# DeltaNet followed by a capacity-limited top-1 expert layer: another way to order the tokens that every expert keeps

## The chip, the cores and the metric

The kernel runs on one core of one Trainium2 chip. The metric is the time of one execution in device microseconds. The kernel before was run three times: the median is 389.66 us (388.7 to 393.39). The profiled execution, from which all times of single instructions below are taken, has a span of 383.6 us.

## The reference

```python
# attention: q, k, v of (4, 8, 768, 48), beta of (4, 8, 768)
k_n = k / (norm(k) + 1e-6)
for t in range(S):                       # a recurrence over 768 steps per head
    y[:, :, t] = q_t @ state
    state = state + beta_t * outer(k_t, v_t - k_t @ state)
x = y as rows (3072 tokens, 384 columns)

# experts: w_gate (384, 8), w1 (8, 384, 1024), w2 (8, 1024, 384), capacity 80
logits = x @ w_gate
expert_idx = argmax(logits, axis=1)
probs = softmax(logits);  gate_w = probs[n, expert_idx[n]]
out = zeros
for e in range(8):
    tok_idx = where(expert_idx == e)
    if len(tok_idx) > capacity:          # keep the 80 with the largest gate_w
        tok_idx = tok_idx[argpartition(-gate_w[tok_idx], capacity)[:capacity]]
    h = maximum(x[tok_idx] @ w1[e], 0)
    out[tok_idx] = gate_w[tok_idx, None] * (h @ w2[e])
```

So each expert serves at most 80 tokens, those whose gate value is largest. Which tokens they are is known only when the last chunk of the recurrence has given the last logits.

## The kernel before

The recurrence runs in 12 chunks of 64 steps (j = 0 to 11). The 3072 tokens lie in 24 columns of 128. The first 16 columns (NS = 16, chunks 0 to 7) are sorted while the recurrence runs, which gives 80 kept candidates per expert ("old", tile AO with one column of values per expert). The last 8 columns (NN = 8) are "new": 4 of them early (chunks 8 and 9), 4 late (chunks 10 and 11). In the end the rank of each token among all of its expert is counted: old against old, old against new, new against old, new against new. The counts are sums of 0/1 tiles, taken on TensorE into PSUM (S_ps).

The gate of a group of columns, on VectorE (or GpSimd for the early group), with the exponential as a polynomial:

```python
def gate(m0, nm, g=nc.vector):
    ...                                   # max, shift, one-hot of the expert, range reduction
    ex = tile_(full, F32, "ex")
    g.tensor_scalar(ex, r, 1.0 / 5040.0, None, op0=Alu.mult)
    for f in (720.0, 120.0, 24.0, 6.0, 2.0, 1.0):
        stt(out=ex, in0=ex, scalar=1.0 / f, in1=r, op0=Alu.add, op1=Alu.mult)
    stt(out=ex, in0=ex, scalar=1.0, in1=two.bitcast(F32), op0=Alu.add, op1=Alu.mult)
    ...                                   # sum, reciprocal: gw, the gate value
    nc.vector.tensor_tensor(out=og, in0=oh, in1=gw..., op=Alu.mult)   # ohg: value at its expert, else 0
```

Old against old, on GpSimd, and old against new, on VectorE:

```python
            yield wide                    # ABC: AO's values as rows, on 128 partitions
            t2 = sl.tile([cap, E, cap], BF16, name="t2")
            for e in range(E):
                row, one_ = ABC[:cap, e], AO[:, e : e + 1]
                nc.gpsimd.tensor_scalar(t2[:, e], row, one_, None, op0=Alu.is_equal)
                nc.gpsimd.tensor_scalar(t1[:, e], row, one_, None, op0=Alu.is_gt)
            nc.gpsimd.tensor_tensor(out=t2, in0=t2, in1=trl[...]..., op=Alu.mult)
            nc.gpsimd.tensor_tensor(out=t1, in0=t1, in1=t2, op=Alu.add)
            after.append(lambda: nc.vector.tensor_reduce(rankO, t1, axis=AX, op=Alu.add))
            yield from against_old(early, ABC, sl)

        def against_old(ms, ABC, sl):
            for m in ms:
                G = sl.tile([128, E, cap], BF16, name="G", bufs=4)
                nc.vector.tensor_tensor(out=G, in0=ABC, in1=ohg[:, NS + m, :]..., op=Alu.is_lt)

                def sums_(m=m, G=G):
                    junk = sl.tile([128, E * cap], BF16, name="junk")
                    nc.scalar.activation(junk, G..., Act.Copy, accum_out=less[:, m : m + 1])
                    for e in range(E):
                        nc.tensor.matmul(S_ps[:cap, 1, 384 + e : 385 + e], lhsT=G[:, e, :], rhs=ones_b[:, 0:1], ...)
                counted.append(sums_)
```

New against new compares one column m with the four columns of a group, which GB holds as rows; equal values inside the own column are settled by the triangle tri:

```python
        def beats(eng, m, ms, GB, sl, own=True):
            ...
            if a:                eng.tensor_scalar(H[:, :a], GB[:, :a], g, None, op0=Alu.is_lt)
            if b < 128 * L:      eng.tensor_scalar(H[:, b:], GB[:, b:], g, None, op0=Alu.is_le)
            if b > a:            # own column: tie, then less-than plus tie
                ...
        def count(m, ms):                 # a matmul of 8 columns for each of the four
            ...
```

The last chunk and the stage after it:

```python
            if j == NC - 2:
                ...
                nc.scalar.copy(GB1, bcast_new(early))
                for m in early:
                    drain(beats(nc.gpsimd, m, early, GB1, s1))
                gate_pool(NS, NN // 2)    # rhs: the products that are gathered later
        ...
        sums(NC - 1)                      # the last logits
        for m in early:
            count(m, early)
        for f in counted:
            f()
        ...
        for i in range(WFIRST):           # 7 of 16 weight tiles
            load_w(i)
        ab, GB1 = bcast_old(), s2.tile(...)
        for h in range(2):
            nc.scalar.copy(ABC[:, 4 * h : 4 * h + 4], ab...)
        nc.scalar.copy(GB1, bcast_new(early))
        drain(gate(NS + NN // 2, NN // 2))
        gate_pool(NS + NN // 2, NN // 2)
        nc.scalar.copy(GB2, bcast_new(late))
        for m in late:
            drain(beats(nc.vector, m, early, GB1, s2))
            count(m, early)
        drain(against_old(late, ABC, s2))
        for f in counted + after:
            f()
        for m in early + late:
            drain(beats(nc.vector, m, late, GB2, s2))
            count(m, late)
        nc.vector.scalar_tensor_tensor(out=slotO, in0=S_ps[:cap, 1, 384 : 384 + E], scalar=1.0, in1=rankO, ...)
        ...                               # slots, indices idx_g and idx_s
    for e in range(E):
        gather(e)                         # rows of x by index, on GpSimd's queue
    for i in range(WFIRST, WR):           # 3 more weight tiles, once tokens are gathered
        load_w(i, ...)
    ...                                   # eight experts: w1, relu, w2, transposed back, scattered
```

PSUM tiles of this part come from `mtile()`, which hands out three buffers in rotation. The program order of each engine is the order of these calls.

Of the kernel before, what the change touches and what calls it, by code (L numbers as in the profile page):

```python
# [1 line left out]

# [18 lines left out]
ROUND = 12582912.0  # L21


@with_exitstack
def kernel(
# [126 lines left out]
    rankO = keep.tile([cap, E], F32, name="rankO")  # L152
    t1 = keep.tile([cap, E, cap], BF16, name="t1")
# [3 lines left out]
    trl = const.tile([128, 128], BF16, name="trl")  # L157
    nc.gpsimd.memset(trl, 1.0)
    nc.gpsimd.affine_select(out=trl, in_=trl, compare_op=Alu.is_gt, fill=0.0, base=0, pattern=[[-1, 128]], channel_multiplier=1)
    ioti = const.tile([128, cap], I32, name="ioti")  # L160
# [25 lines left out]
    with ExitStack() as actx:  # L186
# [416 lines left out]
        def gate(m0, nm, g=nc.vector):  # L603
# [49 lines left out]
            g.tensor_scalar(ex, r, 1.0 / 5040.0, None, op0=Alu.mult)  # L653
            yield 0.25
            for f in (720.0, 120.0, 24.0, 6.0, 2.0, 1.0):
                stt(out=ex, in0=ex, scalar=1.0 / f, in1=r, op0=Alu.add, op1=Alu.mult)
                yield 0.25
            stt(out=ex, in0=ex, scalar=1.0, in1=two.bitcast(F32), op0=Alu.add, op1=Alu.mult)
# [5 lines left out]
            nc.vector.tensor_scalar_add(sm, sm, 1e-9)  # L664
# [42 lines left out]
        def bcast_old():  # L707

            ab = mtile()
            for e in range(E):  # L710
                nc.tensor.transpose(ab[:, e // 4, (e % 4) * cap : (e % 4) * cap + cap], AO[:, e : e + 1].to_broadcast([cap, 128]),
                                    ident[:cap, :cap])
            return ab

# [6 lines left out]
        def choose_sorted(sl):  # L721
# [25 lines left out]
            W2 = [sl.tile([E, 2, 128], F32, name=f"W{i}") for i in range(2)]  # L747
# [58 lines left out]
            hots = [sl.tile([128, E, cap], BF16, name="G", bufs=4) for _ in range(NS // E)]  # L806
# [20 lines left out]
            ABC = sl.tile([128, E, cap], F32, name="ABC")  # L827

            def wide():
                ab = bcast_old()  # L830
                for h in range(2):
                    nc.scalar.copy(ABC[:, 4 * h : 4 * h + 4], ab[:, h, : 4 * cap].rearrange("p (e t) -> p e t", t=cap))

            yield wide
            t2 = sl.tile([cap, E, cap], BF16, name="t2")
            for e in range(E):
                row, one_ = ABC[:cap, e], AO[:, e : e + 1]
                nc.gpsimd.tensor_scalar(t2[:, e], row, one_, None, op0=Alu.is_equal)
                nc.gpsimd.tensor_scalar(t1[:, e], row, one_, None, op0=Alu.is_gt)
            nc.gpsimd.tensor_tensor(out=t2, in0=t2, in1=trl[:cap, :cap].unsqueeze(1).to_broadcast([cap, E, cap]), op=Alu.mult)  # L840
            nc.gpsimd.tensor_tensor(out=t1, in0=t1, in1=t2, op=Alu.add)
            after.append(lambda: nc.vector.tensor_reduce(rankO, t1, axis=AX, op=Alu.add))
            yield from against_old(early, ABC, sl)

        counted, after = [], []

        def against_old(ms, ABC, sl):

            for m in ms:
                G = sl.tile([128, E, cap], BF16, name="G", bufs=4)  # L850
                nc.vector.tensor_tensor(out=G, in0=ABC, in1=ohg[:, NS + m, :].unsqueeze(2).to_broadcast([128, E, cap]), op=Alu.is_lt)

                def sums_(m=m, G=G):
                    junk = sl.tile([128, E * cap], BF16, name="junk")
                    nc.scalar.activation(junk, G.rearrange("p e t -> p (e t)"), Act.Copy, accum_out=less[:, m : m + 1])
                    for e in range(E):
                        nc.tensor.matmul(S_ps[:cap, 1, 384 + e : 385 + e], lhsT=G[:, e, :], rhs=ones_b[:, 0:1], start=False,
                                         stop=(m == NN - 1), skip_group_check=True)

                counted.append(sums_)  # L860
                yield 0.85

        def beats(eng, m, ms, GB, sl, own=True):

            L = len(ms)
            H = sl.tile([128, NN // 2 * 128], BF16, name="H", bufs=4)[:, : 128 * L]
            g = gwN[:, m : m + 1]
            a = sum(i < m for i in ms) * 128
            b = a + 128 * (m in ms)
            if a:  # L870
                eng.tensor_scalar(H[:, :a], GB[:, :a], g, None, op0=Alu.is_lt)
                yield 0.4
            if b < 128 * L:
                eng.tensor_scalar(H[:, b:], GB[:, b:], g, None, op0=Alu.is_le)
                yield 0.4
            if b > a:
                t = sl.tile([128, 128], BF16, name="tie", bufs=2)
                if eng is nc.vector:
                    eng.scalar_tensor_tensor(out=t, in0=GB[:, a:b], scalar=g, in1=tri, op0=Alu.is_equal, op1=Alu.mult)
                    yield 0.3  # L880
                    eng.scalar_tensor_tensor(out=H[:, a:b], in0=GB[:, a:b], scalar=g, in1=t, op0=Alu.is_lt, op1=Alu.add)
                    yield 0.3
                else:
                    eng.tensor_scalar(t, GB[:, a:b], g, None, op0=Alu.is_equal)
# [407 lines left out]
```

## Time and profile before

| | |
|---|---|
| median of three runs | 389.66 us |
| span of the profiled execution | 383.6 us |
| busy: PE, DVE, ACT, POOL | 317.6, 210.0, 178.0, 211.7 us |
| last logits copied (lg) | 268.4 us |
| first weight load issued | 271.7 us |
| slots of the kept tokens (slotO) | 294.4 us |
| first gather | 299.3 us |
| last scatter issued | 379.3 us |

PE is TensorE's matmul, PEld its weight load, DVE VectorE, ACT ScalarE, POOL GpSimd. In the profile's lines, a row gives the start, the duration, the engine, the line of the kernel, the operation, what it writes and reads with shapes, the number of instructions merged into the row, and in brackets the idle time of the engine before it and what ended it. A row of waits gives who waited for whom, the time in total, how many times, and the longest. In the table of slices each digit is the busy share of a fortieth of the span in tenths.

### The profile page before, as it was taken

The numbers are of one execution on the slowest core, as the hardware profiler recorded it, in microseconds if no ns is written. First come the engines' busy times: TensorE is split into PE (matmuls) and PEld (weight loads), VectorE is DVE, ScalarE is ACT, GpSimd is POOL, SyncE is SP. The second block draws the span as 40 slices with busy tenths as digits, with TensorE's granted clock in tenths as the row PEclk, the third lists the DMA queues.
The fourth block names the chain that finished last, engine by engine and source line by source line (L and its number), as shares of the span: only waits on it lengthen the run. The fifth ranks groups of instructions, "written<-read, shape, count | busy, mean of one in ns | idle before, by whom it ended". The sixth has DMA issues, their size and how long they took to land. (4 is left out here: it accounts for less than half of the span.)

```text
span 383.6 us, 16917 instructions
## 1 busy us (share of the span) xinstructions
PE 317.6 (83%) x7356; PEld 280.6 (73%) x7356; DVE 210.0 (55%) x533; ACT 178.0 (46%) x362; POOL 211.7 (55%) x513
## 2 busy tenths in 40 slices
PE   8757869899898999798999898978633699796993
PEld 4544568799798988788999788867532399686893
DVE  7958775676247585599435769696649101010110
ACT  3644347576577676474776666553430011111110
POOL 8540786487775757582776384649994611010010
PEclk9998999899999999899999999898555889999999
DMA  9999548887897969665866566351799616999410
GB/s 139 169 165 180 98 65 167 134 169 120 172 143 152 186 104 169 120 128 103 146 109 142 86 181 138 137 192 48 281 392 388 245 43 222 394 396 392 150 26 17
DMA packets 185257, 65.29 MB, mean 170 GB/s; under 512 B 164160, under 2 KB 181568, under 8 KB 185184
## 3 DMA queue, kind: packets, MB, share of 16 engines
q1 hardware_dynamic: 156144, 56.28, 61.6%
q10 hardware_dynamic: 28272, 5.98, 8.2%
q0 software_dynamic: 768, 1.97, 1.7%
q8 instruction: 58, 0.95, 1.0%
q14 instruction: 15, 0.12, 0.1%
HBM read 44.35 MB, written 19.86 MB: 167 GB/s over the span
## 5 line engine op out<-in xcount | busy, mean ns | idle before, releaser
L415 POOL TENSOR_TENSOR tmpTrue<-XY,NT 128x14 f32<-128x14 f32 (+6 forms) x154 | 44.6, 289 | 12.1
L417 POOL TENSOR_TENSOR XY<-XY,tmpTrue 128x14 f32<-128x14 f32 (+6 forms) x154 | 41.8, 272 | 12.1
L1229 POOL DMA_INDIRECT out_dram<-y,idx_s x8 | 7.4, 921 | 63.4 <-DVE y L1228 63.4
L241 PE MATMUL pm<-SB,KQ 128*64 128x96 f32 x704 | 34.4, 249 | 2.0 <-issue 0.8
L410 POOL TENSOR_TENSOR XY<-NT,eye 128x256 f32<-128x256 f32 x11 | 9.4, 853 | 47.6 <-DMA NT<-a_blocks 42.2
L1237 PE MATMUL hp<-xTe,w 128*64 128x80 f32 x768 | 31.7, 241 | 3.9 <-issue 3.4
L539 DVE TENSOR_TENSOR UB<-pm,beta_t 64x768 f32<-64x768 f32 x24 | 22.9, 954 | 20.2 <-PE pm L241 20.0
L1237 PEld LDWEIGHTS hp<-xTe,w 128*64 128x64 f32 x768 | 29.4, 143 | 5.7 <-issue 5.0
L241 PEld LDWEIGHTS pm<-SB,KQ 128*64 128x64 f32 x704 | 30.6, 138 | 4.0 <-PE pm L241 1.9
L381 DVE TENSOR_TENSOR B<-pm,bm 128x512 f32<-128x512 f32 x24 | 16.3, 681 | 28.7 <-PE pm L241 11.6
L1228 DVE TENSOR_SCALAR y<-yp,gw_t 80x384 f32<-80x384 f32 x8 | 4.9, 613 | 49.0 <-PE yp L1226 49.0
L1250 ACT ACTIVATE hT<-hp 128x320 f32<-128x320 f32 x16 | 7.0, 437 | 52.8 <-PE hp L1237 52.8
L1237 PE MATMUL tp<-hT,w 128*64 128x80 f32 x768 | 29.6, 234 | 2.2 <-issue 1.7
L1237 PEld LDWEIGHTS tp<-hT,w 128*64 128x64 f32 x768 | 27.5, 137 | 3.8 <-issue 2.2
L241 PE MATMUL pm<-KQ 48*64 48x128 f32 x768 | 25.8, 287 | 5.0 <-ACT KQ L356 4.9
L241 PEld LDWEIGHTS pm<-KQ 48*64 48x64 f32 x768 | 22.7, 141 | 7.2 <-ACT KQ L356 6.0
L356 ACT COPY KQ<-pm 128x512 f32<-128x512 f32 x48 | 24.8, 611 | 4.8 <-issue 4.2
L467 ACT COPY X<-pm 32x256 f32<-32x256 f32 x44 | 16.0, 364 | 22.4 <-PE pm L241 18.1
L444 ACT ACTIVATE YB<-YD,qm 128x256 f32<-128x256 f32 x48 | 20.5, 499 | 11.6 <-DMA YD<-inv_blocks 11.6
L341 POOL TENSOR_TENSOR bm<-beta_t,neg_strict 128x1024 f32<-128x1024 f32 x12 | 22.8, 1900 | 1.2 <-DVE beta_t L954 1.2
L561 ACT COPY SB<-S_ps 48x768 f32<-48x768 f32 x22 | 17.5, 794 | 11.4 <-PE S_ps L241 11.2
L241 PE MATMUL pm<-R,Y 64*64 64x48 f32 x704 | 15.0, 235 | 5.2 <-issue 4.7
(258 smaller groups left out, 741.6 us busy)
## 6 DMA issues: line engine op xcount, KB each, us to landing
w<-in_moe_w_dram SPq DMA_DIRECT2D x16, 1536.0 KB, 15.9
qn<-in_q_dram SPq DMA_DIRECT2D x24, 192.0 KB, 5.4
a_blocks<-B ACTq DMA_DIRECT2D x18, 256.0 KB, 5.2
vin<-in_v_dram SPq DMA_DIRECT2D x24, 192.0 KB, 4.9
x_rows<-x SPq DMA_DIRECT2D x24, 192.0 KB, 4.0
out_dram<-zero SPq DMA_DIRECT2D x12, 384.0 KB, 4.4
kr<-in_k_dram SPq DMA_DIRECT2D x23, 192.0 KB, 4.9
inv_blocks<-XY SPq DMA_DIRECT2D x11, 256.0 KB, 2.8
```

The source lines that it names most:

```text
L241: nc.tensor.matmul(out, lhsT=lhsT, rhs=rhs, start=not acc, stop=not acc, skip_group_check=True)
L341: nc.gpsimd.tensor_tensor(out=bms[c], in0=beta_t[:, c].unsqueeze(2).to_broadcast([128, NB, 64]), in1=neg_strict.unsqueeze(1).to_broadcast( ...
L356: nc.scalar.copy(KQs[c][:, 4 * h : 4 * h + 4, n, :], pt[:, h].rearrange("r (g w) -> r g w", w=128))
L381: nc.vector.tensor_tensor(out=own(B1), in0=pv[:, 0], in1=own(bm), op=Alu.mult)
L410: eng.tensor_tensor(out=X, in0=NT.rearrange("p s t -> p t s"), in1=eye16, op=Alu.add)
L415: eng.tensor_tensor(out=tv, in0=X[:, t + 1 :, t : t + 1].to_broadcast(sh), in1=NT[:, 0:t, t].unsqueeze(1).to_broadcast(sh), op=Alu.mult)
L417: eng.tensor_tensor(out=X[:, t + 1 :, 0:t], in0=X[:, t + 1 :, 0:t], in1=tv, op=Alu.add)
L444: nc.scalar.mul(dst, Yd, w)
L467: copy(X4[hs(e, 32), :, h, e], ps[64 * e + 32 * h : 64 * e + 32 * h + 32, 0, :256].rearrange("r (g w) -> r g w", w=32))
L539: nc.vector.tensor_tensor(out=UB[hs(e), :, e].rearrange("r (g c) d -> r c g d", c=2), in0=ps[hs(e), :, : 8 * D].rearrange("r c (g d) -> r ...
L561: nc.scalar.copy(SB[hs(p, D), :, :, p].rearrange("r (b g) e d -> r b (g e) d", b=2), S_ps[hs(p, D), :, : 8 * D].rearrange("r b (g d) -> r ...
L1237: nc.tensor.matmul(out[r], lhsT=lhsT[:, r], rhs=rhs, skip_group_check=True, **kw)
```

## The change

Four things are changed, all of which concern the choice of the kept tokens.

- *Gate.* The polynomial of the exponential has a lower degree and other coefficients, scaled by a constant that is taken out again in the sum: two instructions fewer on VectorE in every gate.
- *Order of the kept tokens.* The 0/1 tiles `below` (less than; equal, times the triangle) are left apart and summed by one-column matmuls into S_ps. The addition on GpSimd, the reduction rankO on VectorE and the tile trl go. GpSimd makes them in the last chunk, ahead of the gate's products, and it makes only two of the four early comparisons; VectorE makes the other two.
- *Old against new.* In place of comparing every token with the kept values of all eight experts, the row of kept values of the token's own expert is fetched by a product: the token's one-hot column is transposed, and multiplied with the kept values, which are split into three bf16 parts (`parts`) that add up to the f32 value. One compare for four columns and one reduction follow.
- *Ties.* Each comparison of new against new is one full-width compare H; the equal values have a tile T of their own, with the triangle on the own column, and their own counting matmuls.

```diff
+EXP = (722.359314, 722.3593374, 361.1796148, 120.3915103, 30.0992743, 6.049220681)
...
-            g.tensor_scalar(ex, r, 1.0 / 5040.0, None, op0=Alu.mult)
-            for f in (720.0, 120.0, 24.0, 6.0, 2.0, 1.0):
-                stt(out=ex, in0=ex, scalar=1.0 / f, in1=r, op0=Alu.add, op1=Alu.mult)
+            for n, f in enumerate(EXP[:0:-1]):
+                stt(out=ex, in0=ex if n else r, scalar=f, in1=r, op0=Alu.add, op1=Alu.mult)
...
             def wide():
-                ab = bcast_old()
+                ab, ap = mtile(), mtile()
+                for n in range(3):
+                    nc.tensor.transpose(ap[:E, 0, cap * n : cap * n + cap], a5[:, :, 2 + n], ident[:cap, :cap])
+                nc.scalar.copy(parts, ap[:E, 0, : 3 * cap]...)
+                for e in range(E):
+                    nc.tensor.transpose(ab[:cap, ...], AO[:, e : e + 1].to_broadcast([cap, cap]), ident[:cap, :cap])
...
-                nc.gpsimd.tensor_scalar(t2[:, e], row, one_, None, op0=Alu.is_equal)
-                nc.gpsimd.tensor_scalar(t1[:, e], row, one_, None, op0=Alu.is_gt)
-            nc.gpsimd.tensor_tensor(out=t2, in0=t2, in1=trl[...]..., op=Alu.mult)
-            nc.gpsimd.tensor_tensor(out=t1, in0=t1, in1=t2, op=Alu.add)
-            after.append(lambda: nc.vector.tensor_reduce(rankO, t1, axis=AX, op=Alu.add))
-            yield from against_old(early, ABC, sl)
+                nc.gpsimd.tensor_scalar(below[0][:, e], row, one_, None, op0=Alu.is_lt)
+                nc.gpsimd.tensor_scalar(below[1][:, e], row, one_, None, op0=Alu.is_equal)
+            nc.gpsimd.tensor_tensor(out=below[1], in0=below[1], in1=tri[...]..., op=Alu.mult)
+            yield partial(own_kept, early, sl)
+            yield from against_old(early, sl)
+
+        def own_kept(ms, sl):
+            L, ot = len(ms), mtile()
+            for n, m in enumerate(ms):
+                nc.tensor.matmul(ot[:E, 0, 128 * n : 128 * n + 128], lhsT=ohN[:, m, :], rhs=identb, start=True, stop=True)
+            ohT = sl.tile([E, NN // 2 * 128], BF16, name="ohT")[:, : 128 * L]
+            nc.scalar.copy(ohT, ot[:E, 0, : 128 * L])
+            own = owns[ms[0]] = ot[:, 1, : cap * L]
+            for n in range(L):
+                for k in range(3):
+                    nc.tensor.matmul(own[:, cap * n : cap * n + cap], lhsT=ohT[:, 128 * n : 128 * n + 128], rhs=parts[:, k, :], ...)
+
+        def against_old(ms, sl):
+            G = sl.tile([128, NN // 2, cap], BF16, name="own")[:, :L]
+            nc.vector.tensor_tensor(out=G, in0=own..., in1=gwN[:, ms[0] : ms[0] + L]..., op=Alu.is_lt)
+            nc.vector.tensor_reduce(less[:, ms[0] : ms[0] + L], G, axis=AX, op=Alu.add)
+            ...                               # four matmuls of 8 columns instead of 32 of one
...
+            eng.tensor_scalar(H, GB, g, None, op0=Alu.is_le if m < ms[0] else Alu.is_lt)
+            if m in ms:
+                T = sl.tile([128, 128 * L - a], BF16, name=f"T{a}")
+                eng.tensor_scalar(T, GB[:, a:], g, None, op0=Alu.is_equal)
+                eng.tensor_tensor(out=T[:, :128], in0=T[:, :128], in1=tri, op=Alu.mult)
...
+            if j == NC - 1:
+                drain(beats(nc.vector, early[2], early, GB1, s1))
...
-                for m in early:
+                for m in early[:2]:
                     drain(beats(nc.gpsimd, m, early, GB1, s1))
-                gate_pool(NS, NN // 2)
...
+            if j == NC - 1:
+                fill(1)
+                drain(beats(nc.vector, early[3], early, GB1, s1))
+                gate_pool(NS, NN // 2)
         sums(NC - 1)
+        wide = bcast_new(early)
...
-        ab, GB1 = bcast_old(), s2.tile([128, 128 * len(early)], F32, name="GB1")
-        for h in range(2):
-            nc.scalar.copy(ABC[:, 4 * h : 4 * h + 4], ab[:, h, : 4 * cap]...)
-        nc.scalar.copy(GB1, bcast_new(early))
-        drain(gate(NS + NN // 2, NN // 2))
+        nc.scalar.copy(GB1, wide)
+        last_gate = gate(NS + NN // 2, NN // 2)
+        for _ in range(12):
+            next(last_gate)
+        own_kept(late, s2)
+        drain(last_gate)
...
-        for f in counted + after:
+        for f in counted:
             f()
+        for t in below:
+            for x in range(E):
+                nc.tensor.matmul(S_ps[:cap, 1, 384 + x : 385 + x], lhsT=t[:, x, :], rhs=ones_b[:cap, 0:1], ...)
...
-        nc.vector.scalar_tensor_tensor(out=slotO, in0=S_ps[...], scalar=1.0, in1=rankO, ...)
+        nc.vector.tensor_scalar_add(slotO, S_ps[:cap, 1, 384 : 384 + E], 1.0)
```

## The prediction

> **What bounds the kernel now.** I read the page's forty slices first, to find the stage that the change edits, then the busy time by stage, then the waits of that stage, then the instructions in order of time. The chain that ended last is no help here: it stops at the final scatter.
>
> The page, slices of 9.6 us each:
>
> ```profile
> PE   8757869899898999798999898978633699796993
> DVE  7958775676247585599435769696649101010110
> POOL 8540786487775757582776384649994611010010
> PEclk9998999899999999899999999898555889999999
> GB/s 139 169 165 180 98 65 167 134 169 120 172 143 152 186 104 169 120 128 103 146 109 142 86 181 138 137 192 48 281 392 388 245 43 222 394 396 392 150 26 17
> ```
>
> Slices 29 to 31 and part of 32 (from 268 us) are the stage between the last chunk of the recurrence and the experts: PE falls to 3 tenths and its clock to 5 while DVE and POOL work. TensorE does not bound this stage; what ends it is the choice of the kept tokens. The same stage cut at its events:
>
> ```profile
> 268.40:274.10 5.70, 2.54 (x43) 2.28 (x42) 5.04 (x24) 2.26 (x6) 5.33 (x13) 0.58 0.59 195
> 274.10:277.30 3.20, 3.20 (x24) 2.97 (x23) 0.05 (x2) 1.34 (x3) 3.20 (x8) 0.50 1.03 420
> 277.30:282.10 4.80, 3.29 (x41) 2.56 (x40) 4.80 (x8) 2.73 (x6) 4.80 (x5) 0.50 1.05 386
> 282.10:287.60 5.50, 0.72 (x9) 0.60 (x8) 0.07 (x2) 1.18 (x4) 5.42 (x9) 0.50 1.03 393
> 287.60:294.40 6.80, 2.58 (x32) 1.71 (x32) 6.41 (x19) 0.00 (x0) 4.62 (x7) 0.50 1.04 394
> ```
>
> Columns: window and length; busy time of PE, PEld, DVE, ACT, POOL; clock; DMA share; GB/s. DVE is full in rows 1, 3 and 5 and empty in rows 2 and 4. So the path is DVE's own work plus two holes of 3.2 and 5.5 us. The waits name both:
>
> ```profile
> DVE rankO L842 <- POOL t L841: 5.4, 1, 5.4
> ACT ABC L1132 <- PE pm L711: 5.1, 1, 5.1
> DVE H L871 <- ACT GB L1133: 3.1, 1, 3.1
> ```
>
> The second hole ends when POOL delivers the order of the kept tokens among themselves. The first ends when ACT has copied GB1, which stood behind ABC, whose transposes stood in PE's queue behind counts that waited for POOL's comparisons. In order of time:
>
> ```profile
> 268.38 0.18 DVE L599 COPY lg<-pm 128x16 f32<-128x16 f32 x1 [2.09 <-PE pm L597]
> ...
> 277.27 1.86 DVE L871 TENSOR_SCALAR H<-GB,gwN 128x512 bf16<-128x512 f32 x4 [3.15 <-ACT GB L1133]
> ...
> 279.05 3.07 DVE L851 TENSOR_TENSOR G<-ABC,ohg 128x640 bf16<-128x640 f32 x4
> ...
> 287.55 0.81 DVE L842 TENSOR_REDUCE rankO<-t 80x8 f32<-80x640 bf16 x1 [5.43 <-POOL t L841]
> ...
> 294.44 0.16 DVE L1148 SCALAR_TENSOR_TENSOR slotO<-S_ps,rankO 80x8 bf16<-80x8 f32 x1 [0.28 <-PE S_ps L895]
> ...
> 299.27 1.20 POOL L1203 DMA_INDIRECT xg<-x_rows,idx_g  x1 [6.76 <-DVE gw_t L1189]
> ```
>
> From the logits (268.4) to the slots (294.4) are 26.1 us, then 4.8 us to the first gather, then 79.8 us of experts to the last scatter's issue at 379.
>
> **What the Trainium skill says.** "VectorE: DVE Perf Modes", Mode 2×_2P: a single-source f32 operation between SBUF operands runs two elements a cycle, one with two tensors doesn't. The trace agrees: starts lie 0.20 us apart after a 128-wide compare against a scalar and about 0.43 after a 512-wide one, 0.6 ns an element, while the two-tensor compare of 640 takes 0.77, 1.2 ns an element. "GPSIMD Engine Reference", Key points: GpSimd shares its SBUF interfaces with VectorE and suffers from two-port or two-input DVE instructions. It agrees: POOL's 80x80 compares take 0.48 us alone and up to 1.65 beside DVE's compares; so work taken from DVE helps POOL too. "TensorE: Matmul & The Clock Gate", What's actually happening: an idle TensorE drops to half clock. It agrees, 0.50 from 274 to 299; I cost added matmuls at the pitch of that stage. "DMA: Bandwidth & Descriptors", Issuing engines are not separate DMA queues: gathers interleave with the weight stream. The first gather, issued under the stream, landed after 5.3 us against a median of 3.1.
>
> **The change part by part.**
>
> 1. *Order of the kept tokens.* The 16 compares on POOL remain but come before the gate's products, as soon as ABC exists (262.8), and not after them (274.2). POOL's own list shrinks before that: of the new tokens' comparisons only m = 0 and 1 stay with it, two times a 512-wide compare (estimate 1.6, from 1.29 for 384 and 0.93 for 256), T of 512 and 384 (1.6, 1.3) and 0.43 for the mask: 7 us, from 255.2 to about 262 where it now ends at 272.2. Then 16 x 0.48 + 1.4 = 9 us, done near 272. The sums go to 16 one-column matmuls at about 0.09 us (32 took 2.95). They are needed near 280. So the 5.43 us hole and the reduction behind it (288.29 - 287.55 = 0.74) go: **-6.17**.
> 2. *GB1.* Its transposes stand ahead of the counts, and no ABC is rebuilt in the last stage. PE and ACT make it during the gate. The hole of 3.15 shrinks to about 0.1: **-3.05**.
> 3. *Kept tokens against new ones.* Four compares of 640 (3.07) become one of 320 from PSUM and one reduction of 320. From the 256-wide PSUM addition (0.42) and the 256-wide reduction (0.42) I estimate 0.5 each: **-2.07**. ACT's four accumulations and 28 of 32 matmuls a group go as well, none on the path. The 12 products with `parts` and 4 transposes (1.3 us on PE) run during the gate.
> 4. *Gate.* Two of 23 instructions at 0.25: **-0.5**.
> 5. *Ties.* The late group's comparisons took 288.29 to 294.44, 6.15. New: 8 compares of 512 (3.45), T of 512, 384, 256 and 128 (0.45 to 0.29, sum 1.45), four products with tri (0.2 each, 0.8), PE's tail 0.4: 6.1. **0.**
> 6. *What it adds on the path.* In the last chunk TensorE does the early group's transposes and products between the output product and the transposes of x. Three transposes of a5 cost 0.5 (0.166 each, as L711). With three PSUM buffers in rotation, the extra buffer puts the product with SB onto the one that DVE's UB still reads until 262.7: it starts at 262.75 and not 261.93, +0.8 which includes the 0.5. Then x is copied (to 266.8), ACT copies ohT behind it (0.59, like GB) to 267.4, twelve products at 0.075 end at 268.3, and only then come the transposes of x, which started at 265.65: **+2.7** on the logits. Two comparisons (m = 2, 3; 1.0 us each) move to DVE, into its idle 1.54 us ahead of UB and into the wait for the logits: free.
>
> Sum: -6.17 - 3.05 - 2.07 - 0.5 + 2.7 = **-9.1 us**. Slots near 285.3, gathers near 290. Weights: the first seven tiles stream until about 302, and the next load was issued at 319.04, after the first scatter (317.85). The gap of 17 us shrinks to 8, so the tail keeps its length and moves whole.
>
> **Rivals.**
> - *PE becomes the bound at half clock*: 26 counts, 12 products, 4 + 8 transposes, some 5 us between the logits and GB2. For it: clock 0.50, in-order queue, and my plan has GB2 only about 0.5 us before its use. Against: PE idles 2 to 4 us in each window above. It would cost 2 to 3: 383.
> - *POOL stays the bound*: the products of the late tokens (rhs) start only with the gate's end and are stretched by DVE, one of them to 3.06 us today. If `below` or rhs comes late, 384 to 387. Against: 6 us of slack.
> - *The gain dies in the tail*: gathers under a full weight stream, then a colder clock in the first expert. For it: the 5.3 us. Against: that delay is already in the old run, and scatters under the stream (392 GB/s) land in 3.7. 382 to 385; whole loss unlikely.
> - *The logits aren't delayed* (part 6 hidden): 377.8.
>
> **Range and chances.** The median before is 389.66, so 380.5; the profiled span of 383.6 should become about 374.5. My uncertainty of the sum is some 3 us and the three times before spread over 4.7, so 376 to 385.5. The 2% line is at 381.9, just above my value: faster 0.68, same 0.30, slower 0.02.
>
> **What would show it.** In the new trace: no DVE wait for POOL ahead of the slots; DVE's wait ahead of the first late-by-early compare under 0.5 us; one 128x320 compare and reduction near 0.5 each; lg copied near 271, not 268.4, with PE waiting for ACT's ohT; slots near 285 and the first gather near 290; from gather to the end 80 us as before. It is wrong if PE or POOL releases DVE after the gate, or if the time from gather to end grows by more than 2 us.

## The result, and the profile after

The kernel after takes 371.02 us (median of 4 runs, 369.18 to 374.43) where the kernel before takes 389.18 (4 runs); the ratio is 0.953 [0.942, 0.963]. Predicted were 380.5, with 385.5 and 376.0 as bounds: the direction was right, the gain was twice as large as predicted. Run again on two chips, the same two kernels gave 0.962 [0.956, 0.967] (called chip A below) and 0.976 [0.969, 0.983] (chip D). That spread is itself part of the answer. The two profiled executions took 385.28 and 374.43 us and so differ by 10.9 us, the medians by 18.2.

The page of the kernel after, in slices of 9.3 us:

```profile
PE   8756978889897998897999899797767599898994
DVE  7968775775336566689462859689396001111110
POOL 8550887687574767575586277437941601010110
PEclk9999899999999999999999999879855689999999
GB/s 147 165 172 193 107 55 173 142 170 116 179 145 147 129 172 143 147 148 91 104 163 112 103 185 53 265 4 213 128 324 414 359 197 230 410 405 407 147 28 15
```

Slices 29 and 30 (270 to 289 us) hold the stage from the logits to the gathers: DVE is at 9 and 6 tenths there. Behind it, the slices in which the weight stream pauses (197 and 230 GB/s) are two, where there were 245, 43 and 222. The stage from the logits to the first gather, cut at its events (columns as before: window, length, busy PE, PEld, DVE, ACT, POOL, clock, DMA share, GB/s):

```profile
268.79:274.19 5.40, 3.23 (x49) 2.79 (x50) 4.81 (x22) 1.16 (x2) 3.87 (x11) 0.50 0.64 211
274.19:275.81 1.62, 1.62 (x21) 1.35 (x18) 1.62 (x5) 0.26 (x1) 1.23 (x4) 0.50 1.02 418
275.81:276.72 0.91, 0.65 (x11) 0.56 (x11) 0.88 (x3) 0.33 (x1) 0.46 (x2) 0.50 1.01 382
276.72:282.48 5.76, 3.85 (x59) 2.92 (x58) 5.34 (x17) 0.00 (x0) 0.00 (x0) 0.50 1.05 413
282.48:287.25 4.77, 3.19 (x21) 1.95 (x22) 3.50 (x15) 0.00 (x0) 0.00 (x0) 0.50 1.05 403
```

DVE is busy in every row. Both rows in which it was empty are gone, and POOL is idle from 276.72 on. The same in DVE's own order of time, with POOL's first gather:

```profile
268.79 0.18 DVE L601 COPY lg<-pm 128x16 f32<-128x16 f32 x1 [0.93 <-PE pm L599]
...
274.20 1.69 DVE L880 TENSOR_SCALAR H<-GB,gwN 128x512 bf16<-128x512 f32 x4
275.81 0.47 DVE L862 TENSOR_TENSOR own<-pm,gwN 128x320 bf16<-128x320 f32 x1
276.32 0.49 DVE L865 TENSOR_REDUCE less<-own 128x4 f32<-128x320 bf16 x1
276.72 2.06 DVE L880 TENSOR_SCALAR H<-GB,gwN 128x512 bf16<-128x512 f32 x5
...
282.48 0.16 DVE L1163 TENSOR_SCALAR slotO<-S_ps 80x8 bf16<-80x8 f32 x1 [0.28 <-PE S_ps L899]
...
287.25 1.19 POOL L1218 DMA_INDIRECT xg<-x_rows,idx_g  x1 [10.92 <-DVE gw_t L1204]
```

The first comparison with GB follows the gate without the wait of 3.15, the compare and the reduction over the token's own expert take 0.47 and 0.49, and nothing stands between the last comparison and the slots but TensorE's 0.28.

To see where the time went I cut the execution at six events: the last R of the recurrence, the slots, the first gather, the first scatter, the last scatter, the end. R is the first tile that VectorE writes in a chunk (the values minus a product with the state); its last one opens chunk 11. The first pair are the two profiles discussed so far. The second and third are pairs on one chip each; on D the kernel before is a version with two storage edits, which is not distinguishable in time (1.003 [0.9995, 1.0064]).

| stretch, us | before | after | A before | A after | D before | D after | predicted change |
|---|---|---|---|---|---|---|---|
| start to last R | 257.75 | 255.91 | 258.19 | 256.04 | 258.38 | 256.00 | 0 |
| last R to slots | 36.69 | 26.57 | 36.86 | 27.58 | 36.81 | 26.25 | -9.1 |
| slots to first gather | 4.83 | 4.77 | 4.85 | 4.77 | 4.82 | 4.75 | 0 |
| first gather to first scatter | 18.58 | 21.21 | 21.86 | 19.21 | 15.12 | 18.75 | 0 |
| first to last scatter | 61.42 | 60.28 | 62.71 | 60.60 | 61.14 | 60.25 | 0 |
| last scatter to end | 6.01 | 5.69 | 6.01 | 5.69 | 5.99 | 5.69 | 0 |
| this run | 385.28 | 374.43 | 390.48 | 373.89 | 382.26 | 371.69 | -9.1 |

The stage that the prediction worked out fell by 10.1, 9.3 and 10.6 us. What it held constant did not stay so: above all the first expert, which changed by +2.6, -2.7 and +3.6, but also the start to the last R (-1.8 to -2.4) and the first scatter to the end (-1.2 to -2.4). The kernel before takes anything from 15.1 to 21.9 there, the kernel after 18.8 to 21.2.

### The profile page after: what moved, and what is told of

It reads as the page before. It is cut to its first block, busy times and chain, and to the rows that moved or that the text cites. A ratio compares the mean times of both kernels' runs of the same rounds, so it can differ in the third digit from the quotient of the medians.

```text
span 372.7 us, 16880 instructions
## 1 busy us (share of the span) xinstructions
PE 317.0 (85%) x7363; PEld 278.7 (75%) x7363; DVE 205.7 (55%) x526; ACT 171.9 (46%) x347; POOL 195.9 (53%) x492
## 5 line engine op out<-in xcount | busy, mean ns | idle before, releaser
L1252 PE MATMUL hp<-xTe,w 128*64 128x80 f32 x768 | 33.1, 245 | 3.8 <-issue 3.3
L1252 PEld LDWEIGHTS hp<-xTe,w 128*64 128x64 f32 x768 | 30.8, 147 | 5.7 <-issue 5.0
L383 DVE TENSOR_TENSOR B<-pm,bm 128x512 f32<-128x512 f32 x24 | 16.3, 683 | 28.9 <-PE pm L243 21.5
L1252 PE MATMUL tp<-hT,w 128*64 128x80 f32 x768 | 30.4, 235 | 1.5 <-issue 0.6
L243 PE MATMUL pm<-KQ 48*64 48x128 f32 x768 | 23.7, 272 | 4.0 <-ACT KQ L358 3.9
L243 PEld LDWEIGHTS pm<-KQ 48*64 48x64 f32 x768 | 20.8, 133 | 6.1 <-ACT KQ L358 4.9
L483 ACT COPY Y<-pm 32x512 f32<-32x512 f32 x22 | 12.7, 578 | 13.5 <-PE pm L243 13.2
```

The lines of the kernel that those rows point to most:

```text
L243: nc.tensor.matmul(out, lhsT=lhsT, rhs=rhs, start=not acc, stop=not acc, skip_group_check=True)
L383: nc.vector.tensor_tensor(out=own(B1), in0=pv[:, 0], in1=own(bm), op=Alu.mult)
L483: copy(Y4[r, :, :, p].rearrange("r a b w -> r (a b) w"), ps[r, 0].rearrange("r (g w) -> r g w", w=32))
L1252: nc.tensor.matmul(out[r], lhsT=lhsT[:, r], rhs=rhs, skip_group_check=True, **kw)
```

## The experiments

My theory at first was the clock: that runs of the kernel before spend more time at TensorE's half clock than its profiled execution did. The rivals were that the selection stage itself varies, that one part (the gate, or GpSimd's order) is worth more than counted, and, later, that the expert stage differs. Each comparison with the kernel before lies on one chip; the chips are called A to D. Times are medians over all runs and ratios are of the fast runs alone (those within 1.5% of the fastest of their kernel), which matters twice: `e_pool`'s profile is of a slow run (386.36 us), and `a_w10`, with one fast run of four (370.32), has no ratio.

### The two kernels again, and two parts alone (chip A)

`b0` is the kernel before, `a0` the kernel after, unchanged.

> The kernel before once more, to see how far its executions differ. Theory clock (the two profiled executions differ by 10.9 us, the medians by 18.2, because the profiled execution of the kernel before had fewer half-clock stretches of TensorE than most others of it): span times one minus the mean granted clock, the time lost to the half clock, is over 28 us in the runs near 388 to 393, against 26.4 in the profiled one of 385.3. Rival (the clock has nothing to do with it, the selection stage itself varies): the lost time stays at 26 +- 1 whatever the time, and the logits-to-slots stretch varies from its 26.1 us.

> The changed kernel once more. Theory clock: times between 368 and 375, and the lost time (span times one minus clock) goes from 16 to 21 us with them, about 1 us of time for 1 us lost. Rival: no such relation; logits to slots is not 13.7 us again.

`b0`: 390.56 us in 22 runs, ratio 1.0005 [0.9975, 1.0035]. Its span times (1 - granted clock) runs from 22.6 to 36.4 us over these executions and goes along with the time (correlation 0.81, 0.5 us for each us): the clock explains a part of the scatter from run to run. But the stretch from the last R to the slots is 36.9 as in the profile that I predicted from (36.7), and in the stage table the profile stands out elsewhere, in the first expert. TensorE's order of time there:

```profile
303.37 0.40 PE L1212 MATMUL xp<-ident,xg 80*128 80x80 f32 x3
304.27 1.94 PE L1237 MATMUL hp<-xTe,w 128*64 128x80 f32 x49 [0.50 <-issue]
306.92 0.36 PE L1237 MATMUL hp<-xTe,w 128*64 128x80 f32 x4 [0.71 <-issue]
308.33 0.40 PE L1237 MATMUL hp<-xTe,w 128*64 128x80 f32 x5 [1.05 <-issue]
309.77 0.55 PE L1237 MATMUL hp<-xTe,w 128*64 128x80 f32 x4 [1.04 <-issue]
311.19 1.09 PE L1237 MATMUL hp<-xTe,w 128*64 128x80 f32 x13 [0.87 <-issue]
```

The first layer, 96 products, breaks into pieces: after 49 products four or five at a time with waits of 0.71, 1.05, 1.04 and 0.87 that no semaphore explains ("issue"). It runs freely again at 311.19; the last packets of the gathers ended at 311.1. In the profile of the kernel before that I predicted from, the same 96 products were one piece of 5.18 us, at a mean clock of 0.67:

```profile
305.79 5.18 PE L1237 MATMUL hp<-xTe,w 128*64 128x80 f32 x96 [0.50 <-DVE xTe L1214]
```

`a0`: 374.14 us, 0.962 [0.956, 0.967]; its first layer is one piece as well:

```profile
295.48 5.25 PE L1252 MATMUL hp<-xTe,w 128*64 128x80 f32 x96 [0.50 <-DVE xTe L1229]
```

Over its six runs the lost time goes from 17.1 to 26.5 us and the time only from 372.9 to 375.4, 0.16 us for each us where the theory expected 1. So neither the clock alone nor the selection stage made the difference that I had to explain; the first expert is in it.

`e_gate`, the kernel before with the shorter gate only:

```diff
-            g.tensor_scalar(ex, r, 1.0 / 5040.0, None, op0=Alu.mult)
-            for f in (720.0, 120.0, 24.0, 6.0, 2.0, 1.0):
-                stt(out=ex, in0=ex, scalar=1.0 / f, in1=r, op0=Alu.add, op1=Alu.mult)
+            for n, f in enumerate(EXP[:0:-1]):
+                stt(out=ex, in0=ex if n else r, scalar=f, in1=r, op0=Alu.add, op1=Alu.mult)
 ...
```

> The kernel before with only the shorter gate. By my sum 0.5 us less, within the noise. Rival loop (the gate also stands in VectorE's way inside the recurrence, where the changed kernel was 1.84 us ahead before the last chunk): 2 us or more, with the recurrence shorter.

388.49 us, 1.004 [0.999, 1.009]: no gain is visible. Last R to slots is 36.8, as without it. What the gate saves is waited for elsewhere: DVE's wait for GB is 5.0 us and not 4.1 as in `b0`, and the one for POOL is still 5.4, because in that kernel GpSimd's delivery ends the stage and not DVE's work. The pieces in the first layer are there too.

`e_pool`, the kernel before with GpSimd's order only: two of the four early comparisons move to DVE, and the gate's products go behind the compares of the kept tokens. No work is taken away.

```diff
+            if j == NC - 1:
+                drain(beats(nc.vector, early[2], early, GB1, s1))
 ...
-                for m in early:
+                for m in early[:2]:
                     drain(beats(nc.gpsimd, m, early, GB1, s1))
-                gate_pool(NS, NN // 2)
 ...
+            if j == NC - 1:
+                fill(1)
+                drain(beats(nc.vector, early[3], early, GB1, s1))
+                gate_pool(NS, NN // 2)
```

> The kernel before with only the moves of GpSimd's work: two of the four early comparisons to VectorE in the last chunk, the products of the early tokens behind the order of the kept tokens. Arithmetic as before. Theory queue (both holes of VectorE, 5.4 and 3.1 us, are GpSimd's late list): both holes go nearly, logits to slots falls from 26 to about 18.5, the time by some 7.5 us against the kernel before. Rival arithmetic (the gain needs the shorter compares and the sums on TensorE): under 3 us.

379.38 us, 0.974 [0.967, 0.981]. Last R to slots is 28.9 and not 36.9: 7.9 of the 9.3 that the whole change brings there, from order alone. Both of DVE's long waits of the kernel before, as in `b0`'s list (engine, what it waited for, us in total, times, longest),

```profile
DVE rankO L842 <- POOL t L841: 5.5, 1, 5.5
DVE H L871 <- ACT GB L1133: 4.1, 1, 4.1
```

are gone from the list of `e_pool` for the same stage, which begins

```profile
DVE lg L599 <- PE pm L597: 0.8, 1, 0.8
DVE AO L823 <- ACT a5f L819: 0.5, 1, 0.5
```

The gathers now land under the weight stream (the first after 6.2 us), and on this chip, where `b0` and `e_gate` break, the first layer of `e_pool` is whole:

```profile
305.81 6.11 PE L1242 MATMUL hp<-xTe,w 128*64 128x80 f32 x96 [0.50 <-DVE xTe L1219]
```

### GpSimd's order undone in the kernel after (chip C)

`a_pool` is the kernel after with all four early comparisons and the gate's products back on GpSimd ahead of the kept tokens' compares (the diff of `e_pool` reversed).

> The kernel after with GpSimd's order undone alone: all four comparisons of the early group on GpSimd again and the gate's products directly behind them, as in the kernel before. Theory 'GpSimd's queue': its list grows by two comparisons with their ties (4 to 6 us) and the 16 compares of the kept tokens fall behind the gate's products; TensorE's sums of them hold the slots up: logits to slots 18 to 20 us and not 13, 379 to 382. Rival 'work removed': what the change takes off DVE and TensorE makes the order unimportant, 374 to 376.

373.15 us, 0.964 [0.957, 0.972]: the rival holds. The kernel after did not run on this chip; its ratio on A is 0.962, so in the whole time no cost of the old order is visible. GpSimd's late list indeed ends at 279.70 (the product with tri), and DVE waits once for what hangs on it:

```profile
DVE own L862 <- PE pm L855: 5.1, 1, 5.1
DVE H L880 <- PE S_ps L899: 3.6, 1, 3.6
```

(the first of the two lies ahead of the logits). But last R to slots is 28.7 against 26.3 to 27.6 with the order as changed (on other chips), 1.0 to 2.4 us. The gains of the parts therefore don't add: order alone brings 7.9, everything else alone 8.1 (36.8 - 28.7), both together 9.3 to 10.6. Each relieves the same bound, GpSimd's delivery, and whichever comes second finds most of it gone.

### What delays the logits (chips B, C and D)

The change puts the early group's transposes and products into the last chunk. TensorE's order of time in the kernel after:

```profile
260.73 1.54 PE L243 MATMUL pm<-SB,KQ 128*64 128x96 f32 x32 [1.66 <-DVE UB L541]
262.07 1.52 PE L243 MATMUL pm<-UB,PT 128*64 128x96 f32 x32
263.52 0.39 PE L849 MATMUL pm<-identb,ohN 128*8 128x128 bf16 x4
265.00 0.60 PE L855 MATMUL pm<-parts,ohT 8*128 8x80 bf16 x12 [1.09 <-ACT ohT L851]
265.53 0.87 PE L589 MATMUL pm<-ident,x 128*128 128x128 f32 x6
```

SB is the state, UB the tile that VectorE makes from R, ohT the turned-round one-hot columns of the early tokens. Two waits were added: 1.66 us until UB has read the PSUM buffer that the product with SB wants, and 1.09 for ScalarE's ohT. In `a_pool`, which has the extra PSUM buffer but not the comparison m = 2 on DVE ahead of UB, the first is 1.27: most of it comes with the buffer, 0.4 with the comparison. From the last R to the logits it is 12.3 to 15.0 us in five profiles of kernels with this order, and 9.2 to 9.3 or 10.6 to 10.7 in those with the old order. In two of the five the product with SB also runs longer (2.11 and 2.73 us instead of 1.54). That is not the change's alone: in `b_pre` and `b_gath`, with the old order and no wait, it takes 2.64 and 2.51, and these are the two with 10.7.

`a_w10` is the kernel after with `WFIRST = 10` in place of 7: ten weight tiles are sent for at once, so that the stream doesn't pause. `a_best` has this, and turns the early group's experts round a chunk earlier, behind GB1, so that the products don't wait for ohT.

> The kernel after with ten weight tiles sent for at once and not seven: the three that waited for the first scatter on GpSimd's queue (sent at 309.6, while the DMA stood idle from 304) follow the first seven without a gap. Theory 'weights': TensorE's waits in the experts behind weights (3.9 us in the profile) go; first transpose to last scatter is 70 to 71 us, time 370 (368 to 371). Rival: the gathers of the later experts and the first scatter land later under the longer stream and hold the first experts up: 374 to 377. Rival: TensorE's own work sets the length, 373 to 374.

> As the ten-tile kernel, and the token's expert of the early group turned round in the chunk before, behind GB1, so that its twelve products don't wait for ScalarE in the last chunk. Theory of the prediction's part 6: the product-to-logits stretch falls by 1.1 (TensorE's wait for ohT) to 2.5 us, the time by as much below the ten-tile kernel: 367.5 to 369. Rival: the x copy and its transposes set the logits, nothing below the ten-tile kernel: 370.

`a_w10`: 376.98 us (4 runs), `a_best`: 374.94, 0.966 [0.960, 0.972]. Both miss what was expected. The weight stream now runs without a gap, and its last tile lands at 346.1 in `a_w10`, where the kernel after has 349.7. But first to last scatter is 62.3, longer than the 60.3 to 61.0 with seven tiles, and TensorE's waits by "issue" in the experts grew from 3.9 to 5.3 us: the weights were not what it waited for. `a_best` loses the wait for ohT and still has logits 12.8 us after R (15.0 in `a_w10`): the wait for UB (1.87 there) remains and the product with SB takes 2.83 us. What the wait for ohT is worth alone does not come out of this run.

`a_logit` takes all three causes away, with seven tiles: besides the earlier turning round,

```diff
-                ab, ap = mtile(), mtile()
+                ab = mtile()
                 for n in range(3):
-                    nc.tensor.transpose(ap[:E, 0, cap * n : cap * n + cap], a5[:, :, 2 + n], ident[:cap, :cap])
+                    nc.tensor.transpose(ab[:E, n // 2, (4 + n % 2) * cap : (5 + n % 2) * cap], a5[:, :, 2 + n], ident[:cap, :cap])
 ...
-            if j == NC - 1:
-                drain(beats(nc.vector, early[2], early, GB1, s1))     # ahead of UB
 ...
-                fill(1)
+                drain(beats(nc.vector, early[2], early, GB1, s1))     # behind UB
                 drain(beats(nc.vector, early[3], early, GB1, s1))
+                fill(1)
```

> The kernel after with three edits in the last chunk: the transposes of a5 share the PSUM buffer of those of AO, so that the product with SB no longer lands on the buffer that DVE's UB still reads; the early tokens' experts are turned round one chunk earlier, so that the products don't wait for ScalarE; and both comparisons on DVE (m = 2, 3) stand behind UB, where DVE is idle for 5 us. Theory: these three are all that delays the logits (12.3 to 15.0 us from the last R in five profiles of kernels after, 9.2 in three of before); they come 9.3 to 10 us after R, slots and gathers move with them, 370.5 (368.5 to 372.5). Rival: the delay comes from TensorE's half clock in that stretch, not from order: 12 to 14 us stay, 373 to 375.

369.72 us, 0.956 [0.948, 0.964], and the logits 9.36 us after R. TensorE's order of time:

```profile
261.23 1.54 PE L243 MATMUL pm<-SB,KQ 128*64 128x96 f32 x32
262.60 1.49 PE L243 MATMUL pm<-UB,PT 128*64 128x96 f32 x32
264.02 0.60 PE L865 MATMUL pm<-parts,ohT 8*128 8x80 bf16 x12
264.67 0.93 PE L589 MATMUL pm<-ident,x 128*128 128x128 f32 x6
```

No wait is left among the four, and the 9.36 us are those of the old order. The three edits were not tried one by one. On chip D it ran beside the kernel after, `a1`:

> The kernel after as it is, on the same chip as the next run: ratio 0.955 to 0.967 to the kernel before, last R to logits 12 to 15 us.

> The kernel after with the three edits for the logits, on the same chip as the kernel after: last R to logits 9.2 to 9.6 us and not 12 to 15, time 2.5 to 4 us below it. Rival: what is gained on the logits is lost behind them (GpSimd's compares of the kept tokens, or the weight stream that starts as early as before), 0 to 1 us.

`a1`: 372.60 us, 0.976 [0.969, 0.983], less of a gain than the 0.955 to 0.967 expected. `a_logit2`: 371.32, 0.966 [0.956, 0.976]. Last R to slots is 23.5 and not 26.3, so 2.8 of the 3 us reach the slots. In this profile they are lost again behind them: the first gather goes 2.2 us earlier (284.84 against 287.00), still under the full weight stream, and the first scatter comes at 306.18 where `a1` has 305.75. The medians differ by 1.3 us and the intervals of the two overlap: a gain in the time is not shown.

### The first expert of the kernel before (chips B, C and D)

`b_warm` is the kernel before with 6 warming products and not 14 ahead of the first expert, `a_warm` the kernel after with 24:

```diff
-        for _ in range(14):
+        for _ in range(6):      # b_warm;  24 in a_warm
```

> The kernel before with 6 warming products ahead of the first expert and not 14. In two of three profiles of the kernel before, TensorE went from the warming products into the first expert without a pause and then stood still four times for about 1 us in the first layer. Theory 'no pause': work of TensorE for over 8 us without a pause brings this on; with 6 products it has 3 us of idle ahead of the first transposes, the first layer runs in one piece (5.2 to 6.1 us), first transpose to last scatter is 74 to 76 us and not 81, and the time is 384 to 387. Rival 'gathers': the gathers that land beside the products hold TensorE up, whatever ran before: the pieces of 4 or 5 products remain, 80 to 81 us, time 389 to 391. Rival 'cold': less warming leaves the first layer at half clock, 390 to 392.

> The kernel after with 24 warming products and not 14, so that they end near 295, when the first gather has landed. Theory 'no pause': the first layer now breaks into pieces as in the kernel before, first transpose to last scatter is 79 to 81 us and not 74, and the time is 378 to 381. Rival 'gathers': they land as late and under the same weight stream as before, nothing changes but the clock of the first layer: 372 to 374.

`b_warm`: 390.29 us, 0.997 [0.994, 1.001]. TensorE was idle for 2.63 us ahead of the first transposes, and the first layer still came in pieces (52, 2, 1, 3 and 38 products; free again at 317.07; the gathers' last packets ended at 316.9). So 'no pause' falls. `a_warm`: 376.87, 0.974 [0.965, 0.983]; one wait of 1.04 us in its first layer, after 42 products, and none behind it.

`b_gath` is the kernel before with the gathers of experts 2 to 7, and the three weight loads behind them, held until the first layer is through ScalarE.

```diff
+        if behind is not None:
+            nc.gpsimd.tensor_copy(xgs[e][:, :1], behind)
 ...
-    for e in range(E):
+    for e in range(2):
         gather(e)
 ...
+            if e == 0 and f1 == FK:
+                for g in range(2, E):
+                    gather(g, hT[:cap, f0, :1])
```

> The kernel before with the gathers of experts 2 to 7 held until ScalarE has the whole first layer of the first expert (a GpSimd copy into each gather's tile makes them wait). Theory 'gathers': gathers that land while no weight stream runs hold up TensorE's instruction supply; the first layer then runs in one piece, and pieces of 4 products with 1.05 us between them appear in the second layer instead, beside the gathers, or not at all. Rival 'program place': TensorE stands still after some 50 products of the first layer whatever lands then: the pieces stay in the first layer. Time between 386 and 393 either way, as the second expert's tokens come no later.

382.72 us, 0.997 [0.993, 1.002]. No pieces, neither beside the gathers in the second layer nor in the first. But on this chip (C) a kernel with the gathers in their old place, the next one, has no pieces either: nothing follows from it.

`b_pre` is the kernel before with two storage edits of the change that bear on its first 75 us; `b_pre2` is the same on chip D in more runs.

```diff
-        Xbf = blk.tile([128, 512], BF16, name="Xbf")
+        Xbf = vec.tile([128, 512], BF16, name="Xbf", tag="x")
 ...
-    ioti = const.tile([128, cap], I32, name="ioti")
+    ioti = lg.rearrange("p m e -> p (m e)")[:, :cap].bitcast(I32)
```

> The kernel before with the two storage edits of the change that touch the first 75 us: Xbf lives in a buffer of x, ioti in lg. Theory 'storage': they let the recurrence start earlier (first R at 74 to 75 in the kernels after, 75 to 81 in those before), 386 to 388. Rival 'chance': the clock's windows at the start differ from run to run; first R anywhere from 75 to 81, 389.5 to 392.

> The two storage edits (Xbf in a buffer of x, ioti in lg) in the kernel before, in five rounds. Theory 'storage': ratio 0.98 to 0.99, the first substitution on VectorE again starts near 27.4 us (27.1 to 27.7 in kernels after, 28.4 to 29.5 in kernels before) and the gain of 1 to 2 us is still there at the last R. Rival 'chance': ratio 0.995 to 1.005.

`b_pre`: 381.95 us in 4 runs, 0.981 [0.968, 0.994]; `b_pre2`: 383.38 in 22 runs, 1.003 [0.9995, 1.0064]. The second, with more runs, counts: the storage edits don't change the time. Its last R is at 258.38, as in the kernel before. What `b_pre2` does show is the first layer of a kernel before on chip D, under the same conditions as `b0`: first gather 2 us ahead of the stream's end (302.2), landed 3.0 us after its issue.

```profile
303.82 0.40 PE L1212 MATMUL xp<-ident,xg 80*128 80x80 f32 x3
304.71 3.54 PE L1237 MATMUL hp<-xTe,w 128*64 128x80 f32 x96 [0.50 <-DVE xTe L1214]
```

One piece of 3.54 us, at full clock, and the first scatter 15.1 us after the first gather. On this chip the kernel before takes 383.6 us, on C 385.3, on A and B 390.6 and 391.7. The kernel after on chip D has, in the same view,

```profile
293.01 0.40 PE L1227 MATMUL xp<-ident,xg 80*128 80x80 f32 x3 [2.41 <-issue]
293.90 4.97 PE L1252 MATMUL hp<-xTe,w 128*64 128x80 f32 x96 [0.50 <-DVE xTe L1229]
```

a later first gather (landed 5.7 us after its issue; TensorE waits 2.4 us) and a slower first layer, at a mean clock of 0.70.

`b_w10` is the kernel before with `WFIRST = 10`, so that its gathers lie under the stream as those of the kernel after do.

> The kernel before with ten weight tiles sent for at once and not seven, so that the stream runs on past the gathers without its pause of 16 to 22 us. Theory 'stream': the first layer runs in one piece (5.2 to 6.1 us), the first gather to the last scatter takes 81 to 82 us (a ten-tile kernel after: 81.6) and not 83.5 to 84.6, 386 to 388 where the kernel before has 390. Rival: longer gathers under the stream cost what the pause cost, no change.

385.68 us, 1.011 [1.004, 1.019]. The rival is right: the stream no longer pauses, first to last scatter falls to 59.2, but the first gather lands 6.0 us after its issue and the first scatter comes after 20.3 us instead of 15.1. Under the stream the first expert takes 19 to 21 us on every chip and in either kernel; behind the stream's end, 15.1 to 19.4 where the first layer stays whole (21.2 in `b_gath`, whose held gathers stand ahead of the first scatter) and 22 where it breaks.

## Why the prediction was off

**Step by step.** *Order of the kept tokens* and *GB1* (-6.17 and -3.05): both holes went, and DVE doesn't wait for POOL ahead of the slots. The sizes held as a sum, but they belong to no single edit: `e_pool` shows that order alone empties both holes (7.9 of the stage), `a_pool` that the rest without it brings 8.1. *Kept against new* (-2.07, from an estimate of 0.5 for each of two instructions): 0.47 and 0.49. *Gate* (-0.5): 5.40 us from logits to gate's end against 5.70, and worth nothing by itself in `e_gate`. *Ties* (0): 5.76 against 6.15, a gain of 0.4. Logits to slots fell by 12.4 (26.06 to 13.69) where these terms give 11.8.

*Added on the path* (+2.7): R to logits went from 10.63 to 12.88 in the profiled pair, +2.25. Against the 9.2 of most other profiles with the old order it is +3.1 to +5.8. The mechanism was right, its size too small for most profiles: I gave the wait for UB 0.8 and it takes 1.66 to 2.63, partly because the comparison that I called free (m = 2) holds UB up until 258.67, 0.46 us after its input is done at 258.21. Part of the larger figure doesn't count, since the old kernel's slots waited for GpSimd whenever the logits came: R to slots was 36.7 to 36.9 with logits 9.2 or 10.6 us after R (36.2 in `b_w10` alone). The sum for this stage, -9.1, is met by -9.3 to -10.6.

**The step that failed** is "the tail keeps its length and moves whole", and with it the sentence that the median becomes 380.5 because the stage loses 9.1. First gather to first scatter did not keep its length. In the profile that I read it took 18.6 us; on chips A and B it takes 21.9 and 22.1, where the first layer breaks into pieces (9.5 us in `b0`, where mine had 5.18) while the gathers land behind the stream's end. In `a0` and in `e_pool` they land under the stream and the first layer stays whole. First scatter to last, too, went from 61.1 to 62.7 before to 60.3 to 60.6 after. On A the tail shrinks by 4.8 us (84.6 to 79.8 from first gather to last scatter); on chip D, where the old first layer was never broken, it grows by 2.7 (76.3 to 79.0). I added a stage's gain to a median of 389.66 although the profiled execution took only 385.28, and did not ask which stage made the 4.4 us between them. On A the pair's -16.6 is -9.3 in the stage, -5.1 from the first gather to the end and -2.1 ahead of the last R. On chip D, with 382.26 before, the two runs in the table give -10.6 and the ratio of 0.976 gives -9.2: near the predicted gain, but by luck, since -10.6 in the stage and -2.4 ahead of the last R meet +2.4 behind the first gather. A smaller slip in the same step: I let the first seven tiles stream until 302, and they landed by 304.15.

**What stays open.** In all three pairs the recurrence is 1.8 to 2.4 us shorter in the kernel after, in which almost nothing of it was edited. Over all profiles the ranges overlap: the first R is at 73.9 to 75.7 in nine profiles of kernels after and at 74.2 to 80.9 in nine of kernels before, the last R at 252.7 to 258.4 and at 257.2 to 264.4. Storage edits were tried and aren't the cause of it. TensorE's clock in the first 37 us is 1.00 in the three profiles of the kernel after and 0.95 in those of the kernel before in the table; why is not shown. That the pieces go with certain chips is what four chips show with one to three profiles each; that they need gathers behind the stream's end is what the profiles on A and B have in common; their mechanism is not shown. Nor is it known which chip the first comparison ran on: its median before (389.18) is near those of A and B, its median after (371.02) below A's 374.14 and nearer to D's 372.60. Of its 18.2 us, the 7.3 that the profiled pair doesn't have lie in executions without a profile, and their cause stays open; the pair on A, with 16.6 us, shows how most of them can arise.

**The rivals.** TensorE at half clock was not the bound: its clock is 0.50 from logits to slots, but DVE never waited for it longer than 0.28 there. POOL had delivered in time. The third rival, a gain that dies in the tail, holds in part on chip D (+2.4 from the first gather to the end, above the 2 us that I had named as a sign of being wrong) and the reverse on A. That the logits aren't delayed is wrong for the change and true of `a_logit`.

## What to carry to other kernels

A sum of holes and instructions within one stage came within 1.5 us here (-9.1 against -9.3 to -10.6), but parts that relieve the same queue must not be credited one by one: alone they brought 7.9 and 8.1 us, together about 10. If the profiled execution lies some microseconds from the median, find the stage that varies before calling anything behind the change constant. When work is moved into a busy stretch, count which PSUM buffer every later tile falls on: one tile more in a rotation of three came with 1.3 us of waiting, 1.7 to 2.6 with a comparison ahead of the reader, and with the tile shared and the comparison moved the wait was gone.

## What the runs showed of the hardware

TensorE's waits by "issue" inside a layer go along with its own instruction transfers. In `a_w10`, under the full weight stream, such transfers of 16 KB start at 313.5, 319.8, 325.7, 331.6, 337.7 and 344.1, and TensorE goes on after its waits at 315.92, 322.09, 328.02, 334.08, 340.23 and 346.38, each time 2.3 to 2.5 us after the start of the transfer, though the transfer itself is recorded with 0.9 to 1.0 us. Not every transfer has a wait behind it: the one at 300.8, also under the stream, has none. The first of these waits:

```profile
312.02 2.85 PE L1252 MATMUL tp<-hT,w 128*64 128x80 f32 x76
315.92 0.91 PE L1252 MATMUL tp<-hT,w 128*64 128x80 f32 x20 [1.05 <-issue]
```

The Trainium skill, "Runtime: NRT & Kernel Launch", Instruction fetch mechanics, says that the sequencer fetches blocks of 16 KiB over a DMA queue of its own while it executes, and calls the cost mostly hidden. The trace agrees on the size of the blocks; here, with a transfer every 6 us and the weight stream running, the waits add up to 5.3 us in the experts of `a_w10`. That the transfers cause the waits is argued from their timing; no run changed them. Whether the pieces in the first layer on chips A and B have the same root isn't shown: the transfer ahead of them was complete at 305.8 in `b0`, and the first wait began at 306.21.
